# A TensorE transpose for a DMA transpose, and a new order of steps, in a fused linear-attention and expert kernel

## The chip, the cores and the metric

One Trainium2 chip, one core. The metric is device time in microseconds (us) of one launch, lower is better. All runs quoted are of the state "fast", and all gave correct results.

## The reference

Linear attention over 8 batches and 8 heads, whose output is the input of a mixture of 4 experts (two matrix products with a ReLU between them), summed with given weights.

```python
def _attn_ref(q, k, v):                      # (8, 8, 576, 64)
    q_p, k_p = phi(q), phi(k)                # phi(x) = elu(x) + 1
    kv  = einsum('bhsd,bhse->bhde', k_p, v);  z = sum(k_p, axis=2)
    num = einsum('bhsd,bhde->bhse', q_p, kv)
    den = einsum('bhsd,bhd->bhs', q_p, z)[..., None] + 1e-06
    return num / den

def _moe_ref(x, domain_probs, w1, w2):       # x (4608, 512), w1 (4, 512, 1024), w2 (4, 1024, 512)
    p = domain_probs / (domain_probs.sum(-1, keepdims=True) + 1e-09)
    for e in range(E):
        out += p[:, e:e+1] * (maximum(x @ w1[e], 0) @ w2[e])
```

## The kernel before

The tokens go in 9 tiles of 512 (the first 512 of each batch, and one tile of leftovers). For a tile the attention runs in four *pairs* of heads: `phi` of q, k (ScalarE exp, then VectorE), the transpose of q (`pe_qT`), the products k'v (`kv`), numerator and denominator (`nd_pair`, then the division on VectorE, which gives `x`), and the transpose of x (`pe_xT`), which is the input `xT` of layer 1 of the experts. In tile 0 each expert's unit is cut in 16 *pieces* of 4 matmuls of 512 columns: 8 of layer 1, 8 of layer 2. Batch 1's attention is put between the pieces of tile 0.

Two ways to transpose x of one pair:

```python
def pe_xT(self, pair):                       # TensorE, then a ScalarE copy
    ps = aps([P, CM, P], FP16, "psum_xT")
    for c in range(CM):
        nc.tensor.transpose(out=ps[:, c], in_=self.x[:, pair, c], identity=identh)
    nc.scalar.copy(out=self.xT[:, pair], in_=ps.rearrange("p c i -> p (c i)"))

def dma_xT(self, pair):                      # a DMA that transposes
    nc.sync.dma_start_transpose(
        out=self.xT[:, pair].rearrange("p (c i) -> p c i", i=P),
        in_=self.x[:, pair].rearrange("p c i -> p (c i)"))
```

With cuts:

```python
praw = tile_pool(bufs=4)                     # q, k, v as loaded: 4 buffers for 6 loads of a batch
def alloc(self):
    ...                                      # kp, vp, vl, qT, x, xT of a batch
    nc.gpsimd.memset(self.vp[:, :, :, D:DE], 1.0 / SX)      # POOL
    nc.gpsimd.memset(self.vl[:, :, D:DE], 1.0 / SX)         # POOL
def left_kv(self):
    self.left_act("k"); self.left_dve("k")   # VectorE: the leftover rows of k
    self.left_v(nc.gpsimd)                   # POOL: cast into vl
def warm(n):  ...                            # n matmuls of 512 columns whose result nobody reads

# start: weight loads of all experts, then batch 1's loads, all issued on POOL, in this order
for r in range(6): load_w(0, r)
for e in range(1, E):
    for r in range(4): load_w(e, r)
b1.load_left("k", "v", "q", eng=nc.gpsimd)
for n, g in [q0, k0, v0, q1, k1, v1]: b1.load(n, g, nc.gpsimd, ...)
b0.nd_pair(0)
b0.dma_xT(0)                                 # <- pair 0 of batch 0: by DMA
...
b0.pe_xT(1); warm(1); b0.nd_pair(3)
phs = [layer1_group(0, 0, fj, hT, None, range(0, 2)) for fj in range(2)]   # needs xT of pairs 0, 1
b0.pe_xT(2); ...; b0.pe_xT(3)

for i, g in enumerate(pieces):               # the 64 pieces of tile 0
    g[0](*g[1:])
    ... weight_sums(...)                     # VectorE: sums of weight blocks, used from tile 1 on
    while done < len(steps) and T0 + TG * (i + 1) >= steps[done][0]:
        steps[done][1](*steps[done][2:])     # a step of batch 1's attention
        done += 1
```

The program order on each engine is the order of this text; semaphores are made by the framework.

## Time and profile before

| | before |
|---|---|
| median of 3 runs | 522.96 us (521.85 to 523.14) |
| span of the profiled run | 520.5 us |
| TensorE (PE) waits from 18 to 92 us | 6.9 us in four groups |
| layer 1 of tile 0 runs without a gap from | 26.07 us |
| layer 1 of tile 1 runs without a gap from | 90.22 us |

The head of the profile page: busy time of each engine, its share of the span, and the number of instructions.

```profile
span 520.5 us, 9979 instructions
...
PE 498.0 (96%) x3809; PEld 357.7 (69%) x3809; DVE 342.8 (66%) x676; ACT 288.1 (55%) x563; POOL 197.6 (38%) x207
```

PE is busy 96% of the span. Only PE's gaps can be won, and the question is where they are. The list of who waited for whom, for PE alone, from 18 to 92 us (columns: total us, times, longest):

```profile
PE ph L421 <- DMA xT<-x_sb: 3.5, 1, 3.5
PE psum_xT L399 <- DVE x_sb L346: 1.5, 4, 0.7
PE psum_kv L323 <- POOL vp L195: 1.0, 1, 1.0
PE ph L421 <- ACT xT L400: 0.9, 2, 0.5
```

Half of it is one wait of 3.5 us for the DMA that writes xT. The timeline of all engines shows it (columns: start us, duration us, engine, line, operation, out<-in, shape, count; in brackets the idle time before it and what ended that):

```profile
14.02 0.42 DVE L346 TENSOR_TENSOR x_sb<-psum_nd,recip 128x256 f16<-128x256 f32 x1
...
14.47 1.35 SPq L406 DMA_TRANSPOSE xT<-x_sb  x1
...
18.02 0.54 PE L363 MATMUL psum_nd<-kvz_65,qT 128*128 128x130 f16 x4
...
22.10 1.87 PE L421 MATMUL ph<-xT,w_0_72 128*128 128x512 f16 x4 [3.55 <-DMA xT<-x_sb]
...
26.07 5.56 PE L421 MATMUL ph<-xT,w_0_72 128*128 128x512 f16 x25 [0.46 <-ACT xT L400]
```

x of pair 0 is ready at 14.44 (14.02 + 0.42); its DMA goes out at 14.47 and PE is released at 22.10. PE had nothing to do from 18.56. The same transpose is quick elsewhere in this trace: over its 25 issues the median from issue to landing is 2.5 us, and this one, beside the weight loads, is the longest with 7.6. What comes after is slow too: four matmuls take 1.87 us, where the stream from 26.07 has one each 0.216 us. The table by stretch (busy us of PE, PEld = weight loads, DVE, ACT, POOL; then the granted PE clock, the DMA engines' share, GB/s) has the reason:

```profile
20.00:22.00 2.00, 0.00 (x0) 0.00 (x0) 0.05 (x1) 0.00 (x0) 0.61 (x1) 0.89 1.25 200
22.00:24.00 2.00, 1.90 (x7) 0.78 (x7) 0.00 (x0) 0.00 (x0) 0.37 (x2) 0.50 1.24 206
```

The granted clock is 0.50 from 22 to 24 us. In steps of 0.25 us the same table has 1.00 up to 21.50 and from 25.00 on, 0.50 between, and 0.61 and 0.56 in the two steps at the edges, so the clock is halved from about 21.56 to 24.97, for 3.41 us. It falls inside the wait of 3.55 us; what makes it fall and rise is not shown. (The DMA share of 1.24 to 1.25, above 1, means that the times of packets overlap: the weight loads are in flight.)

The second stage is the last unit of tile 0, from 66.22 to 90.22 us. All engines, around the first `kv` of batch 1:

```profile
71.77 0.69 DVE L240 TENSOR_SCALAR kp<-rawb 128x1024 f16<-128x1024 f32 x1
...
72.85 1.05 ACT L246 CAST vp<-rawb 128x1024 f16<-128x1024 f32 x1
73.01 1.71 POOL L186 DMA_DIRECT2D rawb<-in_v_dram  x2 [2.60 <-ACT h L429]
...
74.72 0.26 POOL L195 MEMSET vp<- 128x32 f16 x1
...
75.03 0.39 PE L323 MATMUL psum_kv<-vp,kp 128*128 128x130 f16 x4 [0.99 <-POOL vp L195]
...
90.22 5.56 PE L421 MATMUL ph<-xT,w_0_72 128*128 128x512 f16 x25 [0.46 <-ACT xT L400]
```

PE has finished its pieces and waits 0.99 us for POOL's memset of vp. That memset stands behind the issue of the load of v1 (73.01), and that load waits for a buffer: it goes out 0.55 us after the first half of phi of k0 on VectorE has ended (71.77 + 0.69), and before the cast of v0 has ended (73.90), so the buffer is that of k0.

### The profile page before, as it was taken

To read this page: it belongs to the slowest core of one execution; us is meant where nothing else is said; L and a number is where in the kernel's file an instruction comes from. 1 tells how busy PE (TensorE), PEld (TensorE's weight loads), DVE (VectorE), ACT (ScalarE), POOL (GpSimd) and SP (SyncE) were. 2 spreads that over 40 slices of the span, in tenths; PEclk is the share of its full clock that TensorE was granted. 3 is DMA by queue.
4 is the path that set the end of the run, shared out by engine and by line. 5 is a ranking of instruction groups with operands and counts; after the bars stand their busy time and mean duration, and the time that the engine had idled before them with its cause. 6 is when DMAs were issued, how large, how long until landed. Compare 5 with 4: busy or idle time off the path is not lost.

```text
span 520.5 us, 9979 instructions
## 1 busy us (share of the span) xinstructions
PE 498.0 (96%) x3809; PEld 357.7 (69%) x3809; DVE 342.8 (66%) x676; ACT 288.1 (55%) x563; POOL 197.6 (38%) x207
## 2 busy tenths in 40 slices
PE   7499998999999999999999999999999999999996
PEld 3244444577777686868686877787867777878783
DVE  5443377488767786768766975698568655655573
ACT  5453374873768366935783578538763354335430
POOL 3522221206442363337333724272607260825150
PEclk9899999999999999999999999999999999999999
DMA  9999924746343525252515362523143010001003
GB/s 269 196 206 208 258 82 134 188 166 141 103 147 86 118 70 169 62 130 66 191 61 122 45 201 82 116 49 102 62 47 47 21 61 1 1 33 51 0 2 83
DMA packets 80737, 54.35 MB, mean 104 GB/s; under 512 B 46032, under 2 KB 73680, under 8 KB 80688
## 3 DMA queue, kind: packets, MB, share of 16 engines
q1 hardware_dynamic: 71648, 41.77, 30.3%
q0 software_dynamic: 9040, 11.93, 12.0%
q8 instruction: 30, 0.49, 0.4%
q14 instruction: 19, 0.16, 0.1%
HBM read 45.16 MB, written 9.44 MB: 105 GB/s over the span
## 4 chain that ended last, share of the span: by engine, by line
PE 81%; ACT 6%; DVE 5%; DMA 5%; issue 2%; POOL 0%; SPq 0%; ACTq 0%; DVEq 0%
PE py L476 26%; PE pb L622 18%; PE py L556 15%; PE pe L622 9%; PE ph L421 5%; PE ps L622 4%; DMA xT<-x_sb 2%; ACT ee L226 2%; DMA rawb<-in_k_dram 2%; PE psum_kv L323 1%; ACT qp L228 1%; DVE acc L467 1%; PE psum_nd L363 1%; DVE x_sb L346 1%; PE warm_ps L742 1%
## 5 line engine op out<-in xcount | busy, mean ns | idle before, releaser
L467 DVE SCALAR_TENSOR_TENSOR acc<-py,p_sb,acc 128x256 f32<-128x256 f32 (+1 forms) x230 | 128.8, 566 | 40.4 <-PE py L556 24.3
L530 POOL TENSOR_TENSOR hs<-h 128x512 f16<-128x512 f16 x30 | 34.6, 1154 | 235.0 <-DVE h L606 235.0
L476 PEld LDWEIGHTS <-h 128*128 128x128 f16 x672 | 65.5, 98 | 29.6
L476 PE MATMUL py<-w_1_77,h 128*128 128x512 f16 x288 | 80.6, 379 | 0.0
L476 PE MATMUL py<-w_3_79,h 128*128 128x512 f16 x288 | 79.3, 379 | 0.0
L666 ACT ACTIVATE h<-pb 128x512 f16<-128x512 f32 x62 | 37.1, 599 | 73.6 <-PE pb L622 73.4
L556 PEld LDWEIGHTS <-h 128*128 128x128 f16 x480 | 46.8, 98 | 10.3 <-issue 3.9
L465 ACT ACTIVATE acc<-py,p_sb 128x256 f32<-128x256 f32 (+1 forms) x64 | 32.5, 507 | 12.0 <-PE py L556 6.4
L556 PEld LDWEIGHTS <-hs 128*128 128x128 f16 x360 | 35.2, 98 | 5.1 <-issue 0.9
L226 ACT ACTIVATE ee<-rawb 128x512 f16<-128x512 f32 (+1 forms) x54 | 37.0, 692 | 0.1
L531 POOL TENSOR_TENSOR hs<-hs,h 128x512 f16<-128x512 f16 x30 | 34.6, 1155 | 2.4
L429 ACT ACTIVATE h<-ph 128x512 f16<-128x512 f32 x40 | 23.2, 598 | 21.7 <-PE ph L421 21.5
L533 POOL TENSOR_TENSOR hs<-h,hs 128x512 f16<-128x512 f16 x30 | 34.7, 1156 | 0.0
L532 POOL TENSOR_TENSOR h<-h 128x512 f16<-128x512 f16 x30 | 34.7, 1155 | 0.0
L622 PEld LDWEIGHTS <-w_2_74 128*128 128x128 f16 x256 | 25.0, 98 | 11.6
L622 PEld LDWEIGHTS <-w_1_73 128*128 128x128 f16 x256 | 24.8, 98 | 7.2
L556 PE MATMUL py<-w_2_78,h 128*128 128x256 f16 x192 | 28.6, 272 | 0.1
L622 PEld LDWEIGHTS <-w_3_75 128*128 128x128 f16 x256 | 24.1, 98 | 5.7
L556 PE MATMUL py<-w_0_76,h 128*128 128x256 f16 x168 | 25.2, 272 | 2.7 <-ACT acc L465 2.7
L622 PEld LDWEIGHTS <-w_0_72 128*128 128x128 f16 x224 | 21.7, 98 | 8.8
L346 DVE TENSOR_TENSOR x_sb<-psum_nd,recip 128x384 f16<-128x384 f32 (+2 forms) x52 | 25.2, 486 | 2.2 <-POOL h L532 0.5
L622 PEld LDWEIGHTS <-s_2_83 128*128 128x128 f16 x192 | 18.5, 98 | 7.8
(533 smaller groups left out, 1018.9 us busy)
## 6 DMA issues: line engine op xcount, KB each, us to landing
out_dram<-acc SPq DMA_DIRECT2D x32, 256.0 KB, 2.3
rawb<-in_v_dram SPq DMA_DIRECT2D x13, 512.0 KB, 5.3
rawb<-in_q_dram SPq DMA_DIRECT2D x13, 512.0 KB, 3.9
rawb<-in_k_dram SPq DMA_DIRECT2D x13, 512.0 KB, 4.8
w_0_72<-in_moe_w_dram POOLq DMA_DIRECT2D x4, 256.0 KB, 6.9
w_0_76<-in_moe_w_dram POOLq DMA_DIRECT2D x2, 512.0 KB, 11.3
w_1_73<-in_moe_w_dram POOLq DMA_DIRECT2D x2, 512.0 KB, 15.2
w_1_77<-in_moe_w_dram POOLq DMA_DIRECT2D x2, 512.0 KB, 18.8
```

What stands on the lines that cost most here:

```text
L226: nc.scalar.activation(eeh, src, AF.Exp)
L346: nc.vector.tensor_tensor(out=dst.rearrange("p n (u d) -> p n u d", u=2), in0=ps[:, 0:n, :, 0:D], in1=recip[:, 0:n].broadcast_to([P, n, 2, ...
L465: nc.scalar.activation(acc, ps, AF.Identity, scale=pscal)
L467: nc.vector.scalar_tensor_tensor(out=acc, in0=ps, scalar=pscal, in1=acc, op0=AO.mult, op1=AO.add)
L476: nc.tensor.matmul(out=py, lhsT=rows(hT, fj)[:, ns * P : (ns + 1) * P], rhs=w2_sb[e][:, fj, :], start=(fj == 0), stop=(fj == FC - 1),)
L530: nc.gpsimd.tensor_tensor(out=hs[:, 0], in0=a21, in1=a22, op=AO.add)
L531: nc.gpsimd.tensor_tensor(out=hs[:, 1], in0=hs[:, 0], in1=a11, op=AO.subtract)
L532: nc.gpsimd.tensor_tensor(out=a21, in0=a11, in1=a21, op=AO.subtract)
L533: nc.gpsimd.tensor_tensor(out=hs[:, 2], in0=a12, in1=hs[:, 1], op=AO.subtract)
L556: nc.tensor.matmul(out=ps, lhsT=lhsT(k), rhs=rhs[:, k], start=first and k == 0, stop=k == FH - 1, skip_group_check=True,)
L622: nc.tensor.matmul(out=ps[:, kk], lhsT=lk(kc), rhs=rhs[:, kc], start=first and kk == 0 and kc == 0, stop=kc == 1, skip_group_check=True,)
L666: nc.scalar.activation(self.h[:, :, 1, 0:NH], self.b, AF.Relu)
```

## The change

Its intent: the wait for the DMA goes, as pair 0 is transposed on TensorE like the others; and the steps of batch 1's attention, which were placed by estimated times, are placed by piece numbers, most of them two or three pieces earlier, all within the last unit, so that the pieces cover their latencies.

```diff
         b0.nd_pair(0)
-        b0.dma_xT(0)
         b0.phi("k", 1)
         ...
         b0.pe_qT(2, nc.scalar)
+        b0.pe_xT(0)
+        warm(3)
         b0.kv(2, 1)
         ...
-        T0, TG = 19.5, 0.863
         steps = [
-            (50.0, b1.alloc),            # = after piece 35
-            (61.5, b1.phi, "q", 0),      # 48
-            (62.5, b1.left_kv),          # 49
-            (63.5, b1.phi, "k", 0),      # 50
-            ...
-            (67.0, b1.kv, 0),            # 55
-            ...
-            (72.5, b1.kv, 2, 1),         # 61
+            (36, b1.alloc),
+            (46, b1.phi, "q", 0),
+            (47, b1.left_kv),
+            (48, b1.phi, "k", 0),
+            (49, b1.pe_qT, 0),
+            (50, b1.pe_qT, 1),
+            (50, b1.vcast, 0),
+            (52, b1.kv, 0),
+            (53, b1.phi, "q", 1),
+            (54, b1.nd_pair, 0),
+            ...
+            (60, b1.kv, 2, 1),
+            (60, b1.pe_xT, 1),
+            (61, b1.kv, 3, 1),
+            (62, b1.nd_pair, 2),
+            (63, b1.nd_pair, 3),
         ]
-            while done < len(steps) and T0 + TG * (i + 1) >= steps[done][0]:
+            while done < len(steps) and i >= steps[done][0]:
         ...
         phs = [layer1_group(1, 0, 0, hT, None, range(0, 2))]
-        b1.kv(3, 1)
         phs.append(layer1_group(1, 0, 1, hT, None, range(0, 2)))
-        b1.nd_pair(2)
-        b1.nd_pair(3)
+        b1.pe_xT(2)
         phs.append(layer1_group(1, 0, 2, hT, None, range(0, 2)))
-        b1.pe_xT(2)
-        warm(1)
         b1.pe_xT(3)
```

(The comments with piece numbers are worked out from the old formula.)

More of the change, by code (lines that the diff above doesn't have):

```diff
@@ L797 @@
         b0.pe_xT(3)
-        T0, TG = 19.5, 0.863
         steps = [
-            (20.0, b0.left_q),
-            (20.0, emit_probs),
-            (22.0, b0.dma_qTl),
-            (40.0, b0.nd_left),
-            (50.0, b1.alloc),
-            (61.5, b1.phi, "q", 0),
-            (62.5, b1.left_kv),
-            (63.5, b1.phi, "k", 0),
-            (64.0, b1.pe_qT, 0),
-            (65.0, b1.pe_qT, 1),
-            (65.5, b1.vcast, 0),
-            (67.0, b1.kv, 0),
-            (68.0, b1.phi, "q", 1),
-            (68.5, b1.nd_pair, 0),
-            (69.2, b1.phi, "k", 1),
-            (70.0, b1.nd_pair, 1),
-            (70.5, b1.pe_qT, 2, nc.scalar),
-            (70.8, b1.vcast, 1, 0, 2),
-            (71.0, b1.pe_xT, 0),
-            (71.3, b1.pe_qT, 3, nc.scalar),
-            (71.5, b1.vcast, 1, 1, 2),
-            (72.0, b1.pe_xT, 1),
-            (72.5, b1.kv, 2, 1),
+            (1, b0.left_q),
+            (2, emit_probs),
+            (4, b0.dma_qTl),
+            (22, b0.nd_left),
+            (36, b1.alloc),
[8 more added lines that the diff above has]
+            (54, b1.nd_pair, 0),
+            (55, b1.phi, "k", 1),
+            (56, b1.nd_pair, 1),
+            (56, b1.vcast, 1, 0, 2),
+            (57, b1.pe_qT, 2, nc.scalar),
+            (57, b1.vcast, 1, 1, 2),
+            (58, b1.pe_xT, 0),
+            (59, b1.pe_qT, 3, nc.scalar),
+            (60, b1.kv, 2, 1),
[3 more added lines that the diff above has]
+            (63, b1.nd_pair, 3),
         ]
@@ L839 @@
                 weight_sums2(e - 1, r // 2)
-            while done < len(steps) and T0 + TG * (i + 1) >= steps[done][0]:
+            while done < len(steps) and i >= steps[done][0]:
                 steps[done][1](*steps[done][2:])
                 done += 1
-        for s in steps[done:]:
-            s[1](*s[2:])
         hT = [new_h(), new_h()]
         phs = [layer1_group(1, 0, 0, hT, None, range(0, 2))]
-        b1.kv(3, 1)
         phs.append(layer1_group(1, 0, 1, hT, None, range(0, 2)))
-        b1.nd_pair(2)
-        b1.nd_pair(3)
+        b1.pe_xT(2)
         phs.append(layer1_group(1, 0, 2, hT, None, range(0, 2)))
-        b1.pe_xT(2)
-        warm(1)
         b1.pe_xT(3)
```

## The prediction

> **What bounds it now.** The page's first table has TensorE (PE) busy 96% of the 520.5 us span (chain of waits: 81%). Only PE gaps can be won. By stages: from 0 to 96 us PE is free for 13.9 us; later gaps are small and untouched. Two stages matter:
>
> 1. The start. In the timeline x of pair 0 is ready at 14.44 us; its DMA transpose goes out at 14.47 and lands 7.6 us later (DMA view), since the weight loads hold the DMA engines at a share above 1. PE finishes its last attention product at 18.56 and waits 3.55 us (for DMA xT) until 22.10. Then 512-column matmuls start 0.43 us apart instead of 0.216 until about 25.0. [...] the granted clock (0.50 in 22 to 24 us) agrees. The full stream starts at 26.07.
> 2. The last unit of tile 0 (66.2 to 90.2 us), with batch 1's attention between its pieces. PE loses about 4.4 us: 0.99 at 74.0 (memset of vp on POOL), the rest around pe_xT and its copies, 80 to 83 and 87 to 90.
>
> **What changes.** (1) Pair 0 gets 4 transposes (0.4 us), 3 warm matmuls (0.65) and an ACT copy (0.58). They fit in PE's gap 14.35 to 16.0 and ACT's 15.2 to 16.5; the DMA transpose goes. PE starts layer 1 at about 18.6, warm; the next limit is x of pair 3 (DVE, 19.85), its transposes and copy: stream at about 21.1 instead of 26.07. **Gain about 4.9 us.** Weights land in time, if closely (second half of w2 of expert 0 at about 26.1, wanted at 27.3).
>
> (2) The attention steps come two to three pieces earlier (a piece is 0.864 us).  The first kv moves from piece 55 to piece 52, but its release moves less: the memset of vp stands on POOL behind the load of v1, which waits for the buffer of k0, read by phi k on DVE. DVE is busy without a break from 64.7 to 74.6; adding up its work in the new order, phi k starts at 66.2 us and the memset ends at 69.3. PE has finished piece 52 at 66.0. **New wait about 3.3 us at kv** (0.99 before). Three more pieces then fill later waits; xT of pair 3 still ends the stage, at about 85.2 (before: 90.2). Net of part 2: 0, from -1.5 to +2.
>
> [...]
>
> **Predicted:** 522.96 - 4.9 + 0.3 = about 518.3 us, 8 in 10 between 516.0 and 520.5. Faster by over 2%: 0.03; within 2%: 0.95; slower: 0.02.
>
> **What would show it.** No DMA xT in the chain; stream from about 21.1; landmarks up to 60 us about 5 us earlier; a PE wait of about 3 us for POOL vp near 66 to 69; 25 uninterrupted layer-1 matmuls from about 85.2; first product of tile 1's expert 1 at about 90.6 (before 95.6); later stages merely shifted.
>
> **What would make it wrong.** Batch 1's loads landing later than PE now wants them (q0 landed at 61.05); DVE catching up, so a short kv wait (515 to 516); a cold clock at the front or at kv (520); a wait at nd_left of batch 1.

The sum came to about 518.3 us (522.96 - 4.9 + 0.3). Two passages are cut from the text: a rule on when the clock halves, and a paragraph that took from this rule a chance of 30% for a half clock after the new wait at kv. The 0.3 us in the sum stands without its ground: I read it as the price of that chance, but the text doesn't say how it was worked out.

## The result, and the profile after

| | before | after |
|---|---|---|
| median | 523.05 us (521.85 to 523.28, 4 runs) | 516.61 us (515.81 to 517.51, 4 runs) |
| span of the profiled run | 520.5 us | 514.0 us |
| layer 1 of tile 0 without a gap from | 26.07 us | 20.50 us |
| layer 1 of tile 1 without a gap from | 90.22 us | 83.82 us |

The ratio is 0.9882, with a 95% interval of 0.9859 to 0.9905. Ratios here are the mean time of one kernel's fast runs over that of the other's of the same rounds, so not quite the ratio of the medians quoted. The time of 516.61 us lies inside the predicted range (516.0 to 520.5), 1.7 us below the point; the gain of 1.2% is clear of the noise and under 2%, as the prediction had it.

The page's head after:

```profile
span 514.0 us, 9987 instructions
...
PE 495.8 (96%) x3815; PEld 356.8 (69%) x3815; DVE 342.5 (67%) x676; ACT 289.0 (56%) x564; POOL 198.0 (39%) x207
```

PE's waits from 18 to 92 us after:

```profile
PE psum_kv L323 <- POOL vp L195: 1.7, 1, 1.7
PE ph L421 <- ACT xT L400: 0.7, 2, 0.5
PE psum_kv L330 <- POOL vl L270: 0.4, 1, 0.4
...
PE psum_xT L399 <- DVE x_sb L346: 0.2, 1, 0.2
```

The DMA has left the list, and the waits for x (1.5 us before) have shrunk to 0.2. The wait of the first `kv` for POOL has grown, from 1.0 to 1.7 + 0.4 us. With one smaller wait (0.3 us) the list adds up to 3.3 us in place of 6.9.

The start in the timeline after:

```profile
14.11 0.40 PE L399 MATMUL psum_xT<-identh,x_sb 128*128 128x128 f16 x4 [0.15 <-DVE x_sb L346]
...
14.34 0.81 PE L742 MATMUL warm_ps<-ql 128*128 128x512 f16 x3
...
17.52 0.40 PE L363 MATMUL psum_nd<-kvz,qT 128*128 128x130 f16 x4
...
17.75 1.20 PE L421 MATMUL ph<-xT,w 128*128 128x512 f16 x4
...
20.50 5.55 PE L421 MATMUL ph<-xT,w 128*128 128x512 f16 x25 [0.28 <-ACT xT L400]
```

The transposes of pair 0 and the three warm matmuls fill PE's gap behind `pe_qT`; layer 1 begins at 17.75, straight behind the last attention product, and the clock holds:

```profile
20.00:22.00 2.00, 1.72 (x8) 0.68 (x7) 0.00 (x0) 1.54 (x4) 0.71 (x1) 1.00 1.26 213
22.00:24.00 2.00, 2.00 (x11) 0.93 (x10) 1.56 (x6) 1.77 (x4) 0.00 (x0) 1.00 1.22 201
```

The second stage after, all engines:

```profile
63.86 1.89 PE L421 MATMUL ph<-xT,w 128*128 128x512 f16 x8
...
64.39 1.05 ACT L246 CAST vp<-rawb 128x1024 f16<-128x1024 f32 x1
...
65.60 0.69 DVE L240 TENSOR_SCALAR kp<-rawb 128x1024 f16<-128x1024 f32 x1
65.73 1.42 POOL L186 DMA_DIRECT2D rawb<-in_v_dram  x2 [2.75 <-ACT vp L246]
...
67.14 0.26 POOL L195 MEMSET vp<- 128x32 f16 x1
...
67.24 0.90 POOL L270 CAST vl<-rl 128x256 f16<-128x256 f32 x1
...
67.45 0.39 PE L323 MATMUL psum_kv<-vp,kp 128*128 128x130 f16 x4 [1.71 <-POOL vp L195]
...
68.19 0.22 PE L330 MATMUL psum_kv<-vl,kl 128*128 128x130 f16 x1 [0.35 <-POOL vl L270]
...
83.82 5.55 PE L421 MATMUL ph<-xT,w 128*128 128x512 f16 x25 [0.46 <-ACT xT L400]
```

The load of v1 goes out at 65.73, while phi of k0 still reads its buffer (65.60 to 66.29) and 0.29 us after the cast of v0 (64.39 to 65.44). The profile names that cast as what released it. So this time it was given the buffer of v0. The further 0.35 us at vl is the cast of vl on POOL, which took 0.90 us here and 0.41 in before; why is not shown. The stage from the first piece of the unit (60.65) to the stream of tile 1 (83.82) takes 23.17 us; before, 66.22 to 90.22, it took 24.00.

The sum by the traces: the start gives 26.07 - 20.50 = 5.57 us and the second stage 0.83, together 6.4 us; the spans, which the page rounds, differ by 6.5, so next to nothing is left for the rest of the kernel. Of the 5.57 us, 0.39 us is there before the first changed instruction: the first division of pair 0 (the product with the reciprocal, which writes x) starts at 13.08 after and at 13.47 before. Over the traces, changed front or not, it starts between 12.84 and 13.76 us, so that part is a run's chance and not the change. (The 11 warm matmuls at the head of the kernel take 4.88 us in before and 4.57 in after; that this is the cause is not shown.)

### The profile page after: what moved, and what is told of

The parts are those of the page before. It is cut to its first block, busy times and chain, and to the rows that moved or that the text cites. A ratio compares the mean times of both kernels' runs of the same rounds, so it can differ in the third digit from the quotient of the medians.

```text
span 514.0 us, 9987 instructions
## 1 busy us (share of the span) xinstructions
PE 495.8 (96%) x3815; PEld 356.8 (69%) x3815; DVE 342.5 (67%) x676; ACT 289.0 (56%) x564; POOL 198.0 (39%) x207
## 4 chain that ended last, share of the span: by engine, by line
PE 85%; ACT 6%; DVE 3%; issue 2%; DMA 2%; POOL 0%; SPq 0%; DVEq 0%; ACTq 0%
PE py L476 27%; PE pb L622 19%; PE py L556 15%; PE pe L622 10%; PE ph L421 6%; PE ps L622 5%; ACT ee L226 2%; PE psum_kv L323 1%; ACT qp L228 1%; PE psum_nd L363 1%; DVE x_sb L346 1%; DMA rawb<-in_v_dram 1%; ACT acc L465 1%; DVE acc L467 1%; ACT u L633 1%
## 5 line engine op out<-in xcount | busy, mean ns | idle before, releaser
L476 PE MATMUL py<-w,h 128*128 128x512 f16 x672 | 183.6, 379 | 0.3 <-DVE acc L467 0.3
L633 ACT COPY u<-pb 128x512 f32<-128x512 f32 x186 | 109.1, 588 | 79.6 <-PE pb L622 79.3
L606 DVE CUSTOM_DVE_ANT_0 h<-pe,u 128x512 f16<-128x512 f32 x124 | 85.3, 688 | 80.4 <-ACT u L633 47.4
L622 PEld LDWEIGHTS <-w 128*128 128x128 f16 x992 | 95.5, 98 | 33.4
L622 PEld LDWEIGHTS <-s 128*128 128x128 f16 x744 | 71.7, 98 | 24.8
L622 PE MATMUL pb<-tt,w 128*128 128x256 f16 x496 | 74.4, 273 | 0.0
L556 PE MATMUL py<-w,h 128*128 128x256 f16 x360 | 53.8, 272 | 2.8 <-ACT acc L465 2.7
L606 DVE CUSTOM_DVE_ANT_0 h<-ps,u 128x512 f16<-128x512 f32 x62 | 42.4, 684 | 6.5 <-PE ps L622 3.4
L421 PE MATMUL ph<-xT,w 128*128 128x512 f16 x160 | 37.3, 379 | 0.8 <-ACT xT L400 0.7
L622 PE MATMUL pb<-tt,s 128*128 128x256 f16 x248 | 37.2, 273 | 0.0
```

The costliest lines, as they stand in the source:

```text
L421: nc.tensor.matmul(out=ph, lhsT=w1_sb[e][:, dc, fj * P : (fj + 1) * P], rhs=xT_of(j)[:, dc], start=(dc == 0), stop=(dc == DC - 1),)
L476: nc.tensor.matmul(out=py, lhsT=rows(hT, fj)[:, ns * P : (ns + 1) * P], rhs=w2_sb[e][:, fj, :], start=(fj == 0), stop=(fj == FC - 1),)
L556: nc.tensor.matmul(out=ps, lhsT=lhsT(k), rhs=rhs[:, k], start=first and k == 0, stop=k == FH - 1, skip_group_check=True,)
L606: nc.vector._custom_dve(TENSOR_ADD_SAT, out=out, in0=ps, in1=u, s0=BIG, s1=0.0)
L622: nc.tensor.matmul(out=ps[:, kk], lhsT=lk(kc), rhs=rhs[:, kc], start=first and kk == 0 and kc == 0, stop=kc == 1, skip_group_check=True,)
L633: nc.scalar.copy(u, self.b)
```

## The experiments

Twelve runs, each with 5 rounds. "Stage 2" is the time from the first layer-1 matmul of the last unit of tile 0 to the 25 gapless layer-1 matmuls of tile 1; it does not depend on how the start went.

| run | first division | layer 1 from | stage 2 | wait at first kv | median us | ratio to before |
|---|---|---|---|---|---|---|
| before | 13.47 | 26.07 | 24.00 | 0.99 | 522.96 | 1 |
| after | 13.08 | 20.50 | 23.17 | 2.06 | 516.61 | 0.9882 |
| front_only | 12.94 | 21.28 | 24.02 | 0.99 | 517.26 | 0.9903 |
| steps_only | 13.06 | 25.55 | 24.39 | 2.07 | 523.59 | 1.0018 |
| steps_warm | 13.10 | 25.37 | 23.18 | 0.27 (rest filled) | 520.96 | 0.9960 |
| warm_fill | 13.76 | 25.79 | 24.01 | 0.99 | 521.10 | 0.9967 |
| idle_transpose | 13.28 | 20.74 | 23.80 | 2.06 | 517.41 | 0.9902 |
| pool_order | 13.47 | 21.04 | 22.57 | 1.61 | 515.67 | 0.9862 |
| sums_early | 13.43 | 20.92 | 22.11 | 1.30 | 515.26 | 0.9858 |
| pool_and_sums | 13.38 | 20.87 | 20.76 | none | 513.67 | 0.9825 |
| k0_buffer | 13.45 | 21.25 | 25.57 | 3.25 | 518.60 | 0.9915 |
| after_again | 12.95 | 20.38 | 23.17 | 2.06 | 517.20 | 0.9890 |

(more_fill and fill_last, built on pool_and_sums, are told below; their streams are cut otherwise.) The wait at the first kv is the sum of PE's idle times before the products with vp and with vl. In steps_only and steps_warm the stream of layer 1 begins at half clock (its 25 matmuls take 6.26 and 6.38 us, against 5.56 in before), so their figures in "layer 1 from" are not comparable with the others. pool_order, sums_early and pool_and_sums ran on another chip than after_again; these are compared with it by stage 2 of the traces.

### front_only and steps_only: which half gives what

Edits: the kernel before with only the lines of the diff on pair 0 of batch 0; and with only the others.

> The kernel before with only the front of the change (pair 0 of batch 0 transposed on TensorE with 3 warm matmuls; steps of batch 1 as before). Theory: the front is worth 4.9 to 5.6 us and the steps about 0.8, so 517.4 to 518.2 us; full layer-1 stream from about 20.5 to 21; from there to 66 us shifted unchanged; wait at the first kv again about 1 us, waits near 80 to 90 as before. Rival (the steps carry the gain, the front only gives PE an earlier start that is lost again at batch 1's loads): 520 or more.

> The kernel before with only the new steps of batch 1; DMA transpose of pair 0 kept. Theory: additive, so 0.5 to 1 us faster than before (about 522.2), stream still from about 26; the wait at the first kv 1.5 to 2.5 us instead of 1, fewer waits after it, 25 layer-1 matmuls of tile 1 from about 89.4 (before 90.2). Rival (the steps only pay because of the earlier front): no change, or slower by up to 1.5 us.

front_only: ratio 0.9903 (0.9886 to 0.9919). Stage 2 takes 24.02 us, as before to 0.02 us; all the gain is made at the start and carried unchanged. The theory held. (In this trace the start itself had bad luck: the clock was 0.50 from 16 to 18 us, so the stream begins at 21.28 in spite of an early first division.) Not separated, here or elsewhere, is what the three warm matmuls do beside the transposes: no run leaves them out. The clock of this trace falls between 14 and 16 us (mean 0.90 there, 0.50 in the 2 us behind), in spite of them.

steps_only: ratio 1.0018 (0.9990 to 1.0045), no gain, against what I expected, and its runs fall apart from 521.13 to 525.84. Its trace shows why. At the start the clock falls between 16 and 18 us (mean 0.69) and is 0.50 from 18 to 20; the four layer-1 matmuls from 21.30 take 1.87 us, and the 25 matmuls behind 25.55 take 6.26 us, where before has 5.56. In the second stage the wait at kv is 2.07 us, as after, but the clock falls after it:

```profile
72.00:76.00 4.00, 2.43 (x16) 1.37 (x17) 2.81 (x6) 1.05 (x4) 1.91 (x5) 0.85 0.39 131
76.00:80.00 4.00, 4.00 (x21) 2.03 (x20) 2.32 (x6) 2.89 (x5) 0.00 (x0) 0.72 0.01 4
```

Eight matmuls behind kv take 3.12 us here; the same eight take 1.89 in the trace of after. What sets this wait of 2.07 us, which lost the clock, apart from the one of 2.06 in after, which did not (1.00 from 64 to 76 us), is not shown. So the new steps by themselves carry the clock risk that I had put at 30%. By this run alone the rival ("worth nothing without the early front") was not refuted; the next run was made for it.

### steps_warm: is it the clock

```diff
+            (52, warm, 8),
             (52, b1.kv, 0),
```

(on top of steps_only: 8 matmuls of 512 columns that nobody reads, inside the wait)

> Steps only (old front, new steps) with 8 warm matmuls (1.7 us) before the first kv, inside PE's wait there. It tells whether steps_only was no faster because its clock halved after the wait at kv. Theory: clock 1.00 throughout the stage, stage 2 from the 16th layer-1 matmul group to the 25 matmuls of tile 1 takes 22.7 to 23.2 us (24.4 in steps_only, 24.0 before), about 522.0 us and runs closer together (steps_only spread over 4.7 us). Rival (the new steps are worth nothing without the early front): 523 or more.

Ratio 0.9960 (0.9936 to 0.9985), 519.25 to 521.46 us. Stage 2 takes 23.18 us, the figure of after to 0.01, and the clock is whole:

```profile
72.00:76.00 4.00, 3.66 (x25) 1.84 (x24) 2.76 (x5) 1.43 (x5) 1.84 (x5) 1.00 0.41 131
76.00:80.00 4.00, 4.00 (x29) 2.21 (x28) 2.95 (x8) 3.88 (x7) 0.00 (x0) 1.00 0.02 4
```

So the new steps together are worth 0.82 us on their own, if the clock holds; which of the moved steps gives it was not separated. steps_only lost that and more to the clock. The median moved further than the stage (1.5 us against before in the same call). In the traces the span is 1.3 us shorter, of which about 0.6 lies behind stage 2; that part is not explained. The timed runs of before have mean granted clocks from 0.987 to 0.996, and the profiled one 0.996, so most of them were longer at half clock than the trace that is read here.

### warm_fill: how much of the start was the clock

```diff
+        warm(16)
         phs = [layer1_group(0, 0, fj, hT, None, range(0, 2)) for fj in range(2)]
```

(kernel before, DMA transpose kept; PE is kept busy while it waits)

> The kernel before with 16 warm matmuls of 512 columns (3.5 us) put into PE's wait for the DMA transpose; nothing else. It tells the share of the half clock from the share of the wait. Theory: the first layer-1 matmul still comes at about 22.1 but runs at full clock, so the stream starts at about 24.6 to 25.0 instead of 26.07: 1.0 to 1.5 us faster than before, about 521.7. Rival (the half clock is no matter, all is the wait): 523.0, same as before.

Ratio 0.9967 (0.9950 to 0.9985): faster by 1.7 us. In the trace the stream starts at 25.79, after a start that was 0.29 us later than that of before. The clock had already dropped before the filler (0.68 in the stretch from 16 to 18 us, 0.50 from 18 to 20), so that the 16 matmuls took 4.00 us and ended at 23.2; the DMA landed at 22.4 (14.76 + 7.6), so they kept layer 1 itself waiting for 0.8 us. What stood behind the filler shows the size of the clock: from the first layer-1 matmul to the stream 2.58 us, where before took 3.97. So about 1.4 us of the cost is the half clock behind the wait and not the wait itself; the expected figure for the mechanism held, that for the landmark (24.6 to 25.0) did not, as the filler was too long.

### idle_transpose: the wait or the traffic

```diff
         b0.nd_pair(0)
+        spare = px.tile([P, NT], FP16, tag="spare", name="spare")
+        nc.sync.dma_start_transpose(
+            out=spare.rearrange("p (c i) -> p c i", i=P),
+            in_=b0.x[:, 0].rearrange("p c i -> p (c i)"))
```

(kernel after; nobody reads the spare tile)

> The changed kernel, which also issues the DMA transpose of pair 0 at its old place into a spare tile that nobody reads. Theory (the gain is the wait, not the DMA traffic): 516.6, same as after within 0.4 us, weights landing at most 0.5 us later. Rival (taking the transpose out of the busy DMA engines is what speeds the start): back by 1 us or more, 517.6 to 519.

Ratio 0.9902 (0.9884 to 0.9919), which lies between the two expectations; after itself had 0.9882 and, on this chip later, 0.9890. By time (0.2 to 0.8 us more than after) it is inconclusive. The trace shows that the traffic isn't free once PE is early. It has two waits that after has not:

```profile
PE psum_qT L311 <- DVE qp L241: 0.6, 1, 0.6
PE py L476 <- DMA w<-in_moe_w_dram: 0.4, 1, 0.4
```

PE meets the second half of w2 of expert 0 before it has landed (0.4 us), and batch 1's q0 lands later, so the first transposes of q wait 0.6 us. The load of v0 is issued at 59.76 us (after: 58.24; the eight other traces with pair 0 on TensorE: 58.0 to 58.5). So the theory held for the larger part, but taking the transpose out of the busy DMA engines seems to be worth something as well: the two waits are 1.0 us in this one trace.

### pool_order, sums_early, pool_and_sums: what holds the first kv

Edits on the kernel after. pool_order lets POOL issue k1's load after the memsets and v1's after the cast of vl:

```diff
-        for n, g in ORDER:
-            b1.load(n, g, nc.gpsimd, parts=2 if (n, g) == ORDER[-1] else 1)
+        for n, g in ORDER[0:4]:
+            b1.load(n, g, nc.gpsimd)
         ...
             (36, b1.alloc),
+            (37, b1.load, "k", 1, nc.gpsimd),
         ...
             (48, b1.phi, "k", 0),
+            (48, b1.load, "v", 1, nc.gpsimd, 2),
```

sums_early moves the sums of the weights of experts 2 and 3 from pieces 41 to 49 into pieces 34 to 41, where VectorE has 7 us of nothing to do:

```diff
-            if (e, r) in ((2, 14), (2, 15), (3, 1)):
-                weight_sums(3, (r + 2) % 4 if e == 2 else 2)
-            if r in (9, 11, 13) and e < 3:
+            if e == 2 and r in (2, 3, 4):
+                weight_sums(2, r - 2)
+            elif e == 2 and r in (6, 7, 8):
+                weight_sums(3, r - 6)
+            elif (e, r) == (2, 9):
+                weight_sums(2, 3)
+            if r in (9, 11, 13) and e < 2:
                 weight_sums(e, r // 2 - 4)
-            elif r == 15 and e in (1, 2):
+            elif r == 15 and e == 1:
                 weight_sums(e, 3)
```

> The changed kernel with the last two loads of batch 1 issued later on POOL: k1 after the memsets of vp and vl, v1 after the cast of vl. So the first kv no longer waits for POOL. Theory: the DVE is right behind it (phi of k0 ends at 67.3, the memset at 67.4), so the wait at kv goes from about 2.1 us (1.71 and 0.35) to about 1.6 and the time by 0.3 to 0.6 us: about 516.2. Rival (POOL alone holds kv): the wait goes, 2 us faster, 514.6.

> The changed kernel with the weight sums of experts 2 and 3 moved into DVE's idle stretch of 7 us before piece 41, so that phi of q0 and k0 need not queue behind them. POOL order unchanged. Theory: phi of k0 ends about 2 to 3 us earlier, but POOL still issues the load of v1 ahead of the memset of vp, and that load waits for the buffer of v0 (read by the cast that ended at 65.4), so kv moves little: 0 to 0.5 us faster, about 516.4. Rival (DVE alone holds kv; if the load's buffer is that of k0, as predicted blind, the memset moves with phi): 1.5 to 2 us faster.

> Both edits together. Theory: two causes stand behind one wait, each alone hides the other's removal; together the wait at the first kv (2.1 us) goes, and the 25 layer-1 matmuls of tile 1 start about 2 us earlier, at about 81.8: 1.5 to 2.1 us faster than after, about 514.7. Rival (the stage is bound elsewhere, by x of pair 3 or by the loads of k1 and v1): less than 0.7 us.

Alone, pool_order cuts the wait from 2.06 to 1.61 us, as expected, and it is now VectorE's kp that PE waits for; stage 2 is 0.60 us shorter, 515.67 us. Alone, sums_early cuts it to 1.30 us, still for POOL; stage 2 is 1.06 us shorter, 515.26 us. That is more than the 0 to 0.5 us expected: I had taken it that the load of v1 waits for v0's buffer again, but it went out at 65.28, 0.54 us after the first half of phi of k0 (64.04 + 0.70) and before the cast of v0 had ended (65.69), so it had k0's, as the rival had it, and moved with phi. Both together:

```profile
59.87 0.26 POOL L195 MEMSET vp<- 128x32 f16 x1
...
65.92 0.40 PE L323 MATMUL psum_kv<-vp,kp 128*128 128x130 f16 x4
...
81.78 5.56 PE L421 MATMUL ph<-xT,w 128*128 128x512 f16 x25 [0.46 <-ACT xT L400]
```

(kp is ready as well: its last part ended at 65.86.) PE has no wait at the first kv; stage 2 takes 20.76 us, 2.41 less than after; 513.67 us (513.58 to 513.94), ratio 0.9825 (0.9808 to 0.9842); the expected gain was 1.5 to 2.1 us. Two causes stood behind one wait, about equally late. This is why removing the one that the profile names bought only part.

### k0_buffer: the term that the prediction mis-sized

The blind estimate had 3.3 us for the wait at kv, from a load of v1 that waits for k0's buffer; it got v0's. This kernel forces k0's:

```diff
+        def late_pool(self):                 # after phi of k0, on POOL
+            t = self.raw["k", 0]
+            ...                              # load v1 into t, in two halves
+            self.raw["v", 1] = t
+            ...                              # memsets of vp and vl, cast of vl
-            (47, b1.left_kv),
+            (47, b1.left_k),                 # left_kv without the cast of vl
             (48, b1.phi, "k", 0),
+            (48, b1.late_pool),
```

> The changed kernel with one thing forced: the load of v1 of batch 1 writes into the tile of k0, so it has to wait for phi of k0 (as the blind prediction assumed) and not for the cast of v0 (whose buffer it was given). Memsets and the cast of vl stay behind that load on POOL. Theory (the only mis-sized term of stage 2 is this buffer): the load goes out about 0.55 us after the first half of phi k0 instead of 0.3 us after the cast, some 1.1 us later; the wait at the first kv is 3.0 to 3.4 us in place of 2.1, the stage about 1.0 us longer, 517.4 to 517.8 us (more if the clock halves). Rival (the wait was mis-sized elsewhere, say DVE was faster than added up): under 0.3 us slower than after.

```profile
66.36 0.69 DVE L260 TENSOR_SCALAR kp<-rawb 128x1024 f16<-128x1024 f32 x1
...
67.60 1.41 POOL L215 DMA_DIRECT2D rawb<-in_v_dram  x2 [3.87 <-DVE kp L260]
...
69.01 0.26 POOL L220 MEMSET vp<- 128x32 f16 x1
...
69.32 0.39 PE L343 MATMUL psum_kv<-vp,kp 128*128 128x130 f16 x4 [2.82 <-POOL vp L220]
```

The load goes out 0.55 us after the first half of phi of k0 (66.36 + 0.69), just as it did in the kernel before, and PE waits 2.82 us for vp and 0.43 for vl, 3.25 in all. The blind estimate had 3.3 for vp alone and nothing for vl, so that the sums agree this closely is partly luck. In this trace the clock dropped as well (0.90 and 0.67 in the two stretches of 4 us from 68 us on), so stage 2 is 2.40 us longer than after and not the 1.0 expected: 1.19 for the wait, the rest behind it. The median is 518.60 us, against 517.20 for after in the same call. That is within 0.3 us of the predicted 518.3, but it is no proof of it: the one run with a mean clock of 1.000 took 516.91 us, and the predicted sum has the 0.3 us that I read as the price of the clock.

### after_again

No edit: the kernel after once more, beside the others.

> The changed kernel itself again, to be compared with the others on the same chip and to see its spread: 516.6 us, ratio 0.988, wait at the first kv about 2.1 us, stage 2 23.2 us, stream of layer 1 from 20.5 to 21.1 [...].

Ratio 0.9890 (0.9864 to 0.9916), 515.66 to 517.60 us; wait at kv and stage 2 the same to 0.01 us.

### more_fill and fill_last: the last waits of both stages

PE still waits 0.28 and 0.46 us for the last copy of xT in the two tiles. more_fill (on pool_and_sums) starts a fourth layer-1 group before the last `pe_xT` of each, and moves batch 1's nd_left three slots on; fill_last starts it after the last `pe_xT`, and leaves nd_left.

```diff
-        phs.append(layer1_group(1, 0, 2, hT, None, range(0, 2)))
+        phs += [layer1_group(1, 0, fj, hT, None, range(0, 2)) for fj in (2, 3)]    # more_fill
         b1.pe_xT(3)
+        phs.append(layer1_group(1, 0, 3, hT, None, range(0, 2)))                   # fill_last
```

(and the same in tile 0)

> pool_and_sums and two more small edits: a fourth group of two layer-1 matmuls is started before the last pe_xT of each of the first two tiles, to fill PE's waits there (0.28 and 0.46 us), and nd_left of batch 1 goes three slots later, since PE waits 0.6 us for a DMA transpose there. Theory: each filled wait is worth its length, together 0.8 to 1.2 us: about 512.7. Rival (the waits are given back by the next link, x of pair 3 or the DMA): within 0.3 us of 513.67.

> pool_and_sums with a fourth group of two layer-1 matmuls started after (not before) the transposes of pair 3 in both first tiles, nd_left where it was. The filler now stands in PE's wait for the last copy of xT (0.28 and 0.46 us) instead of ahead of the transposes that the copy waits for, which is where more_fill had put it for no gain. Theory: both waits go, 0.6 to 0.7 us faster than pool_and_sums: about 513.0, ratio 0.981. Rival (a next link gives it back): 513.6, and the 23 matmuls of each tile begin 0.43 us later than in the theory.

more_fill: 513.64 us, ratio 0.9822 (0.9797 to 0.9846), no gain over pool_and_sums. The filler stands ahead of the transposes that the copy waits for, so it pushes the last link away by its own length:

```profile
80.70 0.39 PE L399 MATMUL psum_xT<-identh,x_sb 128*128 128x128 f16 x4
...
81.76 5.12 PE L421 MATMUL ph<-xT,w 128*128 128x512 f16 x23 [0.46 <-ACT xT L400]
```

The wait of 0.46 us is still there. The PE wait at nd_left went, and 0.41 us came back at the next kv, for VectorE's kl. fill_last: 513.86 us, ratio 0.9828 (0.9803 to 0.9852), no gain either. Here both waits for the copy are gone (26 matmuls run through from 80.70), but nd_left gives it back:

```profile
94.03 0.71 PE L380 MATMUL psum_nl<-kvz,ql 128*128 128x130 f16 x4 [2.16 <-DMA ql<-qlp]
```

PE waits 2.16 us for the DMA transpose of ql, and the clock is lower around it (mean 0.91 from 82 to 100 us; the four matmuls behind the wait take 0.71 us, where the same four in tile 0 of more_fill take 0.39). The profiled run is the slowest of its seven (516.38; the others 513.46 to 514.15), so the typical run waits less; how much is not seen. fill_last together with the later nd_left was not run, and stays open.

## Why the prediction was right, and where it was off

- **The start: right.** "Gain about 4.9 us", stream "at about 21.1 instead of 26.07". In pool_order, which happens to start like before (first division at 13.47 in both), the stream begins at 21.04: 5.03 us. In the trace of after it was 5.57, of which 0.39 is the chance of an early start. Its two parts, worked out from pool_order's trace: layer 1 starts 3.81 us earlier (18.29 for 22.10), and gets from its first matmul to the stream in 2.75 us in place of 3.97, at a quicker pace (its first four matmuls take 1.20 us, where before has 1.87 at half clock), which is 1.22 us. front_only shows that nothing of it is lost later.
- **The weights: right.** "Land in time, if closely": after shows no PE wait for them, and idle_transpose, with the loads a little later, shows one of 0.4 us.
- **Part 2, mechanism right, one term too large.** I wrote that "the memset of vp stands on POOL behind the load of v1, which waits for the buffer of k0", "new wait about 3.3 us at kv", "net of part 2: 0". The chain is the right one, but the load was given the buffer of v0, whose reader ends earlier (65.44 and not 66.29), and the wait was 2.06 us. Part 2 gained 0.83 us (steps_warm alone: 0.82). k0_buffer puts the assumed buffer back and gets 3.25 us (2.82 for vp, 0.43 for vl). The term that failed is the choice of a buffer, which the framework makes anew for each program: the trace of before showed k0's, sums_early and pool_and_sums got k0's again, after and pool_order v0's (by when the load went out).
- **"Three more pieces then fill later waits; xT of pair 3 still ends the stage": right.** The waits for x fell from 1.5 to 0.2 us, and the last wait of 0.46 us for the copy of xT ends the stage in both.
- **The clock risk: real, but not in the trace of after.** I gave it 30%, an estimate, not shown; the 0.3 us in the sum I read as its price, though the prediction doesn't say so. steps_only and k0_buffer show a lower clock after waits of 2.07 and 3.25 us (0.72 from 76 to 80 us, 0.67 from 72 to 76); both traces of after don't, with 2.06 us (1.00 from 64 to 76). Of the ten timed runs of after (after and after_again) four have a mean clock of 0.994, and took 517.03 to 517.58 us; the others have 0.997, and took 515.66 to 517.60, most of them under 517. One more stretch at half clock, if as long as the 3.41 us in the trace of before, would lower the mean of 514 us by 0.003 (my estimate from these figures), so those four may have lost the clock once more; where is not recorded.

The sum, by the traces: predicted net gain 4.6 us (4.9 - 0.3); 0.8 more from part 2, 0.3 not paid for the clock, 0.7 more at the start (0.4 of it chance) make 6.4, as measured. So about a quarter of the 1.7 us between the point and the result was a lucky start of the profiled run.

## What to carry to other kernels

In some traces here a wait of TensorE cost its length and then a stretch at half speed: 1.2 us behind the 2.07 us in steps_only, 1.4 behind the 3.55 us at the start of before, and nothing behind the 2.06 us in after. So a wait can be worth more than the wait list says, and a step that moves a wait forward can lose by it. When a load stands in front of a small memset in an in-order queue, ask which buffer it will get (here k0's or v0's, for 3.25 or 2.06 us of PE wait), and don't assume that it is the one of the last program: look for the reader whose end came just before the issue. And when a wait is named after one engine, look how far behind the next one is: here removing either cause gave 0.6 to 1.1 us of the stage, and both gave 2.4.
